# Linear attention and a maxout layer on one core: batch 0 reordered, w2 @ w_out by one Strassen level, copies and relus moved to ScalarE

## The chip, the cores and the metric

The kernel runs on one core of one Trainium2 chip. The metric is the device time in microseconds (us) of one execution, the median of several. The core has five engines with queues of their own, each working through its instructions in order: TensorE (PE: matmuls, and loads of their weights, PEld), VectorE (DVE), ScalarE (ACT), GpSimd (POOL, here issuing loads) and SyncE (SP, issuing stores and transposing transfers). They wait for each other through semaphores.

## The reference

```python
# q, k, v: (8, 8, 1024, 64) f32;  E, F: (64, 1024);  w1, w2: (512, 1024);  w_out: (1024, 512)
k_proj = einsum('ks,bhsd->bhkd', E, k)
v_proj = einsum('ks,bhsd->bhkd', F, v)
scores = q @ k_proj^T / 8
attn   = softmax(scores)                       # over 64 projected keys
x      = (attn @ v_proj) -> (8192, 512)        # heads side by side
g      = maximum(x @ w1, x @ w2)               # (8192, 1024)
out    = g @ w_out                             # (8192, 512)
```

## The kernel before

The maxout is rewritten. With wd = w1 - w2 it is max(x @ w1, x @ w2) = relu(x @ wd) + x @ w2, and so

    out = relu(x @ wd) @ w_out + x @ (w2 @ w_out)

The product m = w2 @ w_out (512 x 512) is formed once. Each batch is two units of 512 tokens. For a unit there is an "up" product x @ wd, then a relu, and a "down" product [g, x] @ [w_out; m]. All down products, and the up products from unit 2 on, are computed by one level of Strassen's method (the Winograd form): a 2 x 2 block product with 7 block products in place of 8, and sums of blocks before and after, made by DVE. Batch 0's up products are plain matmuls. Everything runs in f16 with f32 accumulation in PSUM.

The instructions are recorded in an order that the kernel fixes itself. Batch 0, as it stands at the head:

```python
    step_dn(t, 0, 1)              # sums of exp(scores), then Ln on ACT
    step_inv(t, 0, 0)             # Exp(-ln): the reciprocal
    step_inv(t, 0, 1)
    warm(4)                       # 4 matmuls of 512 columns that keep the PE clock up
    step_qt(t, 4, 4, 0, NI // 2)  # transposes of q on PE, copy on DVE
    step_qt(t, 4, 4, NI // 2, NI)
    warm(2)
    step_sc(t, 1, 0)              # scores on PE, Exp on ACT
    step_sc(t, 1, 1)
    step_kv(t, 0, 4, "v")         # projection of the first half of v
    step_dn(t, 1, 0)
    step_at(t, 0, 0)              # values on PE, times the reciprocal on DVE: x
    step_dn(t, 1, 1)
    step_at(t, 0, 1)
    step_inv(t, 1, 0)
    step_kv(t, 4, 8, "v", True)
    step_inv(t, 1, 1)
    step_wd(0, 0, 2)              # wd = w1 - w2, a first piece, on DVE
    step_at(t, 1, 0, True)
    u0, u1 = [*up_slots(t, 0)], [*up_slots(t, 1)]
    step_wd(0, 2, 4)
    step_at(t, 1, 1, True)
    for u in u0, u1:
        for x in u[0:2]:
            x(r1=2)               # first half of the contraction of four up products
```

Then come the up products of batch 0, the transposes of w2 and the product m:

```python
    # in up(): 4 matmuls of 512 columns into one PSUM bank, then the relu into SBUF
                if fb < 3 or j and fb > 3:
                    nc.scalar.activation(out=gt[:, fb, :], in_=h_ps, func=ACTF.Relu)
                else:
                    nc.vector.tensor_scalar_max(gt[:, fb, :], h_ps, 0.0)

    def step_w2t(f0):             # 8 transposes into one bank, one copy on ACT
        ps_t = mm_bank(FP16)
        ...
    def step_m(r):                # one of four row blocks of m
        m_ps = mm_bank(n=(1, 2, 0, 3)[r])
        for fb in range(NFB):     # NFB = 8
            nc.tensor.matmul(
                out=m_ps, lhsT=w2t_sb[:, fb, r * 128 : (r + 1) * 128], rhs=wo_sb[:, fb, :],
                start=(fb == 0), stop=(fb == NFB - 1),
            )
        nc.scalar.copy(out=m_sb[:, r, :], in_=m_ps)

    slots = [
        (0, lambda: u0[0](r0=2)), (1, lambda: u0[1](r0=2)), (None, lambda: loads(1, "v", "q", "k")),
        (2, lambda: u1[0](r0=2)), (3, lambda: u1[1](r0=2)),
        (None, wd[1]), (4, u0[2]), (None, wt[0]), (5, u0[3]),
        (None, wd[2]), (None, wt[1]), (6, u1[2]), (7, u1[3]), (None, wt[2]), (None, wt[3]), (8, u0[4]), (9, u0[5]), (None, wd[3]),
        (10, u1[4]), (11, u1[5]), (12, u0[6]), (13, u0[7]),
        (14, u1[6]), (15, u1[7]),
        *((16 + n, lambda n=n: step_m(n)) for n in range(NDC)),     # NDC = 4
    ]
```

Steps of DVE are hung on these slots: sums of blocks of x (`sums_x`) and of g (`sums_g`), differences of blocks of w_out and m (`step_t` into `T_sb`) and of wd (`step_tw`):

```python
    for key, s_, *a in (
        (10, open_box, 1), (11, sums_x, U[0, 0], (2,)), (12, sums_x, U[0, 0], (0,)),
        (13, sums_x, U[0, 0], (1,)), (14, sums_x, U[0, 0], (3,)), (15, open_box, 0, 2),
        (15, sums_g, U[0, 0], (0, 1)), (16, step_t, 0), (16, sums_g, U[0, 0], (2, 3)),
        *((17 + i // 3, step_tw, i) for i in range(4)), (19, open_box, 3),
    ):
        at_slot((0, key), s_, *a)
```

A unit's down product comes in seven parts p1 to p7 of 12 matmuls of 256 columns, in unit 0 cut into two pieces each. Banks X, Y and Z hold the partial results. Some are copied to SBUF (`keep`), some are read from PSUM by an addition on DVE whose result is stored:

```python
        def keep_d(bank):         # unit 0: on VectorE; other units: on ScalarE
            return keep("pd", bank, *([nc.vector.tensor_copy] if u["n"] == 0 else []))
        def p1(): st["s1"] = keep_d(whole(1, "X", xbank))
        def p2(): add(0, 0, whole(2, "Y", ybank), st["s1"])
        def p6(): st["u1"] = keep_d(whole(6, "X", None))       # goes on in bank X
        def p5(): st["s5"] = keep_d(whole(5, "Z", ybank))      # takes Y's bank: needs p2's addition done
        ...
```

Batch 1's attention (projection of k and v, transposes, scores, sums, values) is hung on the pieces of unit 0, that of later batches on those of later units. From batch 2 on, q is transposed by transfers that SyncE issues. The loads of the batch after next are held back by a one-element copy on GpSimd (`step_gate`) that waits for such a transfer.

Of the kernel before, what the change touches and what calls it, by code (L numbers as in the profile page):

```python
# [16 lines left out]
def kernel(  # L17
# [12 lines left out]
    nc = tc.nc  # L30
# [146 lines left out]
        t["qt"] = qtp.tile([128, H, HALF], FP16, tag="qt", name="qt_sb")  # L177


    def step_kv(t, h0=0, h1=H, which="kv", att=False, dma=False):  # L180
        kv_ps = att_banks()[:, 0, :] if att else mm_bank()
        n = (h1 - h0) * D
        both = which == "v"
        for c in range(NC):
            for w in which:
                i = "kv".index(w)
                for r in range(2) if both else (i,):
                    nc.tensor.matmul(  # L188
                        out=kv_ps[r * KP : (r + 1) * KP, 0:n],
                        lhsT=eft[:, i, c, :],  # L190
                        rhs=t[w][:, h0:h1, c, :],
                        start=(c == 0), stop=(c == NC - 1),
                    )
        fl = lambda ap: ap[:, h0:h1].rearrange("p h z d -> p (h z d)")
        zd = lambda ap: ap.rearrange("p (h d z) -> p h z d", d=D // 2, z=2)
        if "k" in which:
            eng = nc.vector.tensor_copy if which == "k" else nc.scalar.copy
            kp = t["kp"][:, h0:h1]
            eng(out=kp[:, :, 0, :], in_=kv_ps[0:KP, 0:n].rearrange("p (h d) -> p h d", d=D))
        if both:  # L200
            eng = nc.scalar.copy if att else nc.vector.tensor_copy
            eng(out=t["vp"][:, h0:h1], in_=zd(kv_ps[:, 0:n]))
        elif "v" in which:
            def finish_v():
                nc.vector.tensor_copy(out=t["vp"][KP:128, h0:h1], in_=zd(kv_ps[KP:128, 0:n]))
                if dma:
                    nc.vector.tensor_copy(out=kp[:, :, 1, :], in_=kp[:, :, 0, :])
                    step_kpt_dma(t)
                nc.vector.tensor_copy(out=fl(t["vp"][0:KP]), in_=fl(t["vp"][KP:128]))

            if att:
                return finish_v
            finish_v()
# [110 lines left out]
        ld = t["ld", g, j]  # L324
        nc.scalar.activation(out=ld, in_=ld, func=ACTF.Exp, scale=-1.0)

    def step_at(t, g, j, att=False):
        if "xt" not in t:
            new_xt(t)
        ld = t.pop(("ld", g, j))  # L330
        if att:
            both = att_banks()
            at_ps = [both[:, o, :] for o in range(2)]
        else:
            at_ps = [mm_bank() for _ in range(2)]
        values_into(t, g, j, at_ps)
        for o in range(2):
            nc.vector.tensor_tensor(
                out=x_out(t, g, j)[:, :, o, :],
                in0=at_ps[o].rearrange("q (z n) -> q z n", z=2),  # L340
                in1=ld[:, o, None, :].broadcast_to([128, 2, W]),
                op=ALU.mult,
            )
# [63 lines left out]
    def up_slots(t, j):  # L407
        t["gt", j] = gt = gpool.tile([128, NFB, HALF], FP16, tag="gt", name="gt_sb")
        for fb in range(NFB):
            def up(fb=fb, r0=0, r1=NDC):  # L410
                if r0 == 0:
                    t["up", j, fb] = mm_bank()
                h_ps = t["up", j, fb]
                for r in range(r0, r1):
                    nc.tensor.matmul(  # L415
                        out=h_ps,
                        lhsT=wd_sb[:, r, fb * 128 : (fb + 1) * 128],
                        rhs=t["xt"][:, r, :, j * W : (j + 1) * W],
                        start=(r == 0), stop=(r == NDC - 1),
                    )  # L420
                if r1 < NDC:
                    return
                if fb < 3 or j and fb > 3:
                    nc.scalar.activation(out=gt[:, fb, :], in_=h_ps, func=ACTF.Relu)
                else:
                    nc.vector.tensor_scalar_max(gt[:, fb, :], h_ps, 0.0)
            yield up
# [5 lines left out]
            in1=w2_sb[:, r0:r1, f0 : f0 + 256], op=ALU.subtract,  # L433
        )

    def step_w2t(f0):
        ps_t = mm_bank(FP16)
        for f in range(2):
            for r in range(NDC):
                nc.tensor.transpose(  # L440
# [5 lines left out]
        nc.scalar.copy(  # L446
            out=w2t_sb[:, fb : fb + 2, :].rearrange("q f m -> q (f m)"), in_=ps_t
        )

    def step_m(r):  # L450
        m_ps = mm_bank(n=(1, 2, 0, 3)[r])
        for fb in range(NFB):
            nc.tensor.matmul(  # L453
                out=m_ps, lhsT=w2t_sb[:, fb, r * 128 : (r + 1) * 128], rhs=wo_sb[:, fb, :],
                start=(fb == 0), stop=(fb == NFB - 1),
            )
        nc.scalar.copy(out=m_sb[:, r, :], in_=m_ps)

# [29 lines left out]
    def step_t(part, which=range(4)):  # L490
# [4 lines left out]
            lambda h, c: src[:, h * hs : (h + 1) * hs, c * CH : (c + 1) * CH], which,  # L495
        )

    def s_g(i):
        return box[2].rearrange("q (s n m) -> q s n m", s=4, n=NG)[:, i]

# [20 lines left out]
        return u["gt"][:, h * NG : (h + 1) * NG, j * W : (j + 1) * W]  # L521


    def step_s(u, blk, S, which):
        for i in which:
            x, y, op = (
                (blk(u, 1, 0), blk(u, 1, 1), ALU.add),
                (S(0), blk(u, 0, 0), ALU.subtract),
                (blk(u, 0, 0), blk(u, 1, 0), ALU.subtract),
                (blk(u, 0, 1), S(1), ALU.subtract),  # L530
            )[i]
            nc.vector.tensor_tensor(out=S(i), in0=x, in1=y, op=op)  # L532

    def sums_x(u, which):
        step_s(u, x_blk, lambda i: s_x(i, u), which)
# [87 lines left out]
    def down_steps(u, alone):  # L623
# [49 lines left out]
            nc.vector.tensor_tensor(out=o_sb, in0=two(x), in1=two(y), op=ALU.add)  # L673
            store(j, c, o_sb)

        def keep_d(bank):
            return keep("pd", bank, *([nc.vector.tensor_copy] if u["n"] == 0 else []))

        size = 2 * (NG + NX) // (1 if alone else 2 if u["n"] == 0 else 3)

        def piece(k, name, n, m):
# [3 lines left out]
            return product(k, name, n, 2 * (NG + NX) - size)  # L685

        def p1():
            st["s1"] = keep_d(whole(1, "X", xbank))

        def p2():  # L690
            add(0, 0, whole(2, "Y", ybank), st["s1"])

        def p6():
            st["u1"] = keep_d(whole(6, "X", None))

        def p5():
            st["s5"] = keep_d(whole(5, "Z", ybank))

        def p7():
            st["u2"] = keep_d(whole(7, "X", None))  # L700
            if alone:
                add(1, 1, st["u2"], st["s5"])

# [46 lines left out]
    step_dn(t, 0, 1)  # L750
    step_inv(t, 0, 0)
    step_inv(t, 0, 1)
    warm(4)
    step_qt(t, 4, 4, 0, NI // 2)
    step_qt(t, 4, 4, NI // 2, NI)
    warm(2)
    step_sc(t, 1, 0)
    step_sc(t, 1, 1)
    step_kv(t, 0, 4, "v")
    step_dn(t, 1, 0)  # L760
    step_at(t, 0, 0)
    step_dn(t, 1, 1)
    step_at(t, 0, 1)
    step_inv(t, 1, 0)
    step_kv(t, 4, 8, "v", True)
    step_inv(t, 1, 1)
    step_wd(0, 0, 2)
    step_at(t, 1, 0, True)
    u0, u1 = [*up_slots(t, 0)], [*up_slots(t, 1)]
    step_wd(0, 2, 4)  # L770
    step_at(t, 1, 1, True)
    for u in u0, u1:
        for x in u[0:2]:
            x(r1=2)


    load_all(tiles[1], 1, "k", k)
# [4 lines left out]
    def loads(b, *names):  # L782
# [15 lines left out]

    slots = [
        (0, lambda: u0[0](r0=2)), (1, lambda: u0[1](r0=2)), (None, lambda: loads(1, "v", "q", "k")),  # L800
        (2, lambda: u1[0](r0=2)), (3, lambda: u1[1](r0=2)),
        (None, wd[1]), (4, u0[2]), (None, wt[0]), (5, u0[3]),
        (None, wd[2]), (None, wt[1]), (6, u1[2]), (7, u1[3]), (None, wt[2]), (None, wt[3]), (8, u0[4]), (9, u0[5]), (None, wd[3]),
        (10, u1[4]), (11, u1[5]), (12, u0[6]), (13, u0[7]),
        (14, u1[6]), (15, u1[7]),
        *((16 + n, lambda n=n: step_m(n)) for n in range(NDC)),
    ]
    slots = [((0, n), x) for n, x in slots]

# [3 lines left out]
    for n, key in enumerate(units):  # L813
# [4 lines left out]
            continue  # L818
        pieces = [(("P", n, p, i), x) for p, x in enumerate(downs) for i, x in enumerate(x)]
        ups = [*up_steps(U[units[n + 1]])]  # L820
        for h, (x, y) in enumerate(((5, 1), (1, 2)) if n == 1 else ((2, 2), (2, 3))):
            slots += pieces[:x]
            slots.append((("G", n, h), lambda: None))
            slots += pieces[x : x + y]
# [11 lines left out]


    for key, s_, *a in (
        (10, open_box, 1), (11, sums_x, U[0, 0], (2,)), (12, sums_x, U[0, 0], (0,)),
        (13, sums_x, U[0, 0], (1,)), (14, sums_x, U[0, 0], (3,)), (15, open_box, 0, 2),  # L840
        (15, sums_g, U[0, 0], (0, 1)), (16, step_t, 0), (16, sums_g, U[0, 0], (2, 3)),
        *((17 + i // 3, step_tw, i) for i in range(4)), (19, open_box, 3),
    ):
        at_slot((0, key), s_, *a)


    t = tiles[1]
    at_slot((0, 19), new_attn, t)
    at_slot((0, 19), lambda: turn.__setitem__(slice(None), [2, 3]))
    for n, x in enumerate((  # L850
        "", "", "kv", "", "kpt", "qt00 qt10", "", "sc00 sc10", "qt01", "qt11", "",
        "dn00 in00 dn10 in10", "", "", "at00 AT10 sc01",
    )):
        key = ("P", 0, (n - 1) // 2, (n - 1) % 2) if n else (0, 19)
        for name in x.split():
            if name[0] == "k":
                if name == "kpt":
# [9 lines left out]
                at_slot(key, s_, t, *args, *([True] if name[:2] == "AT" else []))  # L867
        if n in (1, 5):
            at_slot(key, step_t, 1, (0, 1) if n == 1 else (2, 3))
        if 6 <= n < 10:  # L870
            at_slot(key, sums_x, U[0, 1], ((2, 0, 1, 3)[n - 6],))


    t = tiles[2]
    at_slot(("P", 0, 1, 0), new_attn, t)
    at_slot(("P", 0, 1, 0), step_qt_dma, t, 0, H // 2)
    at_slot(("U", 1, 0, 1), step_kv, t, 0, H, "kv", True)
    at_slot(("U", 1, 0, 4), step_kpt, t, 0, H, True)
    at_slot(("G", 1, 0), step_qt_dma, t, H // 2, H)
    at_slot(("U", 1, 0, 6), step_gate, t, "qt", H // 2 - 1)  # L880
    at_slot(("U", 1, 0, 6), loads, 3, "k", "v", "q")

    for b in range(3, B):
# [20 lines left out]
    for n, (b, o) in enumerate(units):  # L904
# [2 lines left out]
        if b == 0:  # L907
            where = ()
        elif n == 2:
            where = (("P", 1, 0, 2), 0), (("P", 1, 1, 0), 1), (("P", 1, 1, 1), 2), (("U", 1, 0, 1), 3)  # L910
        else:
            where = tuple((("U", n - 2, 1, k), i) for k, i in ((6, 2), (3, 0), (4, 1), (5, 3)))
        for key, i in where:
# [48 lines left out]
```

The softmax here doesn't subtract the row's maximum and nothing guards it: scores larger than these inputs give would overflow.

## Time and profile before

| | |
|---|---|
| time, median of 3 runs | 325.81 us (325.14 to 325.97) |
| span of the profiled run | 323.2 us |
| granted TensorE clock | 1.00 |
| matmul of 512 columns in a row of such, start to start (6.91 us / 32) | 0.216 us |
| matmul of 256 columns, four in 0.44 us | 0.109 us |
| ACT copy or relu, 128x512 f32 from PSUM | 0.59 to 0.60 us |
| DVE relu, 128x512 f32 from PSUM | 0.69 us |
| DVE sum or difference, 128x1024 f16 | 0.69 us |
| product m on PE | 40.01 to 46.91 us |

How to read it: the page gives each engine's busy time in the span. Matmuls overlap in a pipeline, so one matmul's own duration (0.273 us for 256 columns) is longer than the distance between two. The chain that ended last is followed back from the last instruction, at each step to what released it; the waits say which engine stood idle until another's instruction or a transfer ended. "issue" is time for which the profile shows no cause.

### The profile page before, as it was taken

The page shows a single profiled execution, that of the slowest core. Times are in us where ns is not written, and L with a number is a line of the kernel's source. Part 1 is how long each engine was busy: PE and PEld are TensorE (multiplying, and loading weights), DVE is VectorE, ACT ScalarE, POOL GpSimd, SP SyncE. Part 2 cuts the span into 40 slices and gives each one's busy share as a digit, 9 for nine tenths or more (in the row PEclk, how much of TensorE's full clock was granted, in tenths as well). Part 3 has the DMA queues.
Part 4 walks back from the last instruction along what each step waited for, and adds up shares of the span by engine and source line. Part 5 has one row for each costly group of instructions (what it writes and reads, how often), then busy time and mean ns, then how long its engine had stood idle before and what let it go on. Part 6 is the DMA issues. An engine that isn't in the chain of part 4 may idle for free.

```text
span 323.2 us, 9033 instructions
## 1 busy us (share of the span) xinstructions
PE 316.0 (98%) x3852; PEld 248.4 (77%) x3852; DVE 236.8 (73%) x420; ACT 203.1 (63%) x364; POOL 41.6 (13%) x65
## 2 busy tenths in 40 slices
PE   8989999999999999999999999999999999999995
PEld 3554457878887888878887888878887888888884
DVE  1365798896867797877967796977967796969572
ACT  1466532667676777667776777657776777764541
POOL 8649002001200300030000300030000000000000
PEclk9999999999999999999999999999999999999999
DMA  8999999999999799699979999689969130312133
GB/s 160 207 196 185 204 204 204 207 203 179 256 216 213 135 203 244 143 177 144 234 147 201 154 211 231 115 180 183 232 130 213 38 100 32 99 34 98 34 121 108
DMA packets 76280, 53.14 MB, mean 164 GB/s; under 512 B 29520, under 2 KB 76112, under 8 KB 76240
## 3 DMA queue, kind: packets, MB, share of 16 engines
q0 software_dynamic: 30976, 28.31, 56.0%
q1 hardware_dynamic: 45264, 24.25, 31.2%
q8 instruction: 30, 0.49, 0.6%
q14 instruction: 10, 0.08, 0.1%
HBM read 57.15 MB, written 16.78 MB: 229 GB/s over the span
## 4 chain that ended last, share of the span: by engine, by line
PE 84%; DMA 9%; DVE 2%; POOL 2%; issue 1%; SPq 1%; ACT 0%; DVEq 0%; POOLq 0%
PE mm_ps L649 43%; PE mm_ps L571 24%; PE att_ps L188 4%; DMA v_sb<-in_v_dram 4%; DMA qt_sb<-q_sb 3%; PE mm_ps L415 3%; PE att_ps L287 3%; PE mm_ps L275 3%; PE mm_ps L453 2%; DMA big<-in_moe_w_dram 2%; POOL q_sb L102 1%; POOL k_sb L102 1%; DVE gt_sb L586 1%; PE mm_ps L246 1%; PE mm_ps L440 1%
## 5 line engine op out<-in xcount | busy, mean ns | idle before, releaser
L542 ACT COPY p_sb<-mm_ps 128x512 f32<-128x512 f32 x172 | 97.2, 594 | 42.0 <-PE mm_ps L571 30.0
L649 PEld LDWEIGHTS <-big 128*128 128x128 f16 x768 | 73.5, 98 | 12.0 <-issue 3.5
L649 PE MATMUL mm_ps<-T_sb,big 128*128 128x256 f16 x576 | 77.9, 273 | 0.0
L586 DVE TENSOR_TENSOR gt_sb<-mm_ps,p_sb 128x512 f16<-128x512 f32 x56 | 38.6, 688 | 45.5 <-PE mm_ps L571 42.7
L571 PE MATMUL mm_ps<-big,big 128*128 128x256 f16 x336 | 50.4, 273 | 0.0
L571 PEld LDWEIGHTS <-big 128*128 128x128 f16 x448 | 43.8, 98 | 5.2
L649 PEld LDWEIGHTS <-gt_sb 128*128 128x128 f16 x384 | 35.8, 98 | 9.9 <-issue 5.4
L649 PE MATMUL mm_ps<-wo_sb,gt_sb 128*128 128x256 f16 x256 | 43.0, 273 | 0.1
L571 PEld LDWEIGHTS <-wd_sb 128*128 128x128 f16 x336 | 32.9, 98 | 3.8
L571 PE MATMUL mm_ps<-xt_sb,wd_sb 128*128 128x256 f16 x224 | 33.6, 273 | 0.0
L364 ACT ACTIVATE ex_sb<-mm_ps 128x512 f16<-128x512 f32 x50 | 27.2, 597 | 10.2 <-PE att_ps L287 8.1
L390 DVE TENSOR_TENSOR xt_sb<-att_ps,ld_sb 128x1024 f16<-128x1024 f32 x26 | 31.7, 1219 | 0.1
L673 DVE TENSOR_TENSOR o_sb<-mm_ps,p_sb 128x512 f32<-128x512 f32 x32 | 21.9, 685 | 7.7 <-PE mm_ps L649 7.7
L649 PE MATMUL mm_ps<-m_sb,xt_sb 128*128 128x256 f16 x128 | 24.4, 273 | 0.0
L238 POOL COPY junk<-qt_sb 1x1 f16<-1x1 f16 x6 | 1.7, 284 | 169.6 <-DMA qt_sb<-q_sb 169.6
L621 ACT ACTIVATE gt_sb<-mm_ps 128x512 f16<-128x512 f32 x28 | 16.8, 600 | 8.7 <-PE mm_ps L571 8.7
L532 DVE TENSOR_TENSOR big<-gt_sb 128x1024 f16<-128x1024 f16 x32 | 21.9, 685 | 0.3
L589 DVE TENSOR_SCALAR gt_sb<-gt_sb 128x512 f16<-128x512 f16 (+1 forms) x56 | 20.4, 365 | 1.9
L649 PE MATMUL mm_ps<-wo_sb,big 128*128 128x256 f16 x128 | 21.5, 273 | 0.0
L649 PE MATMUL mm_ps<-T_sb,gt_sb 128*128 128x256 f16 x128 | 21.5, 273 | 0.0
L649 PEld LDWEIGHTS <-xt_sb 128*128 128x128 f16 x192 | 18.8, 98 | 2.2
L586 DVE TENSOR_TENSOR gt_sb<-p_sb 128x512 f16<-128x512 f32 x28 | 19.1, 682 | 0.0
(88 smaller groups left out, 429.5 us busy)
## 6 DMA issues: line engine op xcount, KB each, us to landing
out_dram<-o_sb SPq DMA_DIRECT2D x63, 256.0 KB, 2.7
k_sb<-in_k_dram POOLq DMA_DIRECT2D x7, 1024.0 KB, 11.3
v_sb<-in_v_dram POOLq DMA_DIRECT2D x7, 1024.0 KB, 16.7
q_sb<-in_q_dram POOLq DMA_DIRECT2D x5, 1024.0 KB, 22.8
q_sb<-in_q_dram POOLq DMA_DIRECT2D x4, 512.0 KB, 19.4
big<-in_moe_w_dram POOLq DMA_DIRECT2D x12, 128.0 KB, 8.6
k_sb<-in_k_dram POOLq DMA_DIRECT2D x4, 256.0 KB, 6.1
q_sb<-in_q_dram POOLq DMA_DIRECT2D x4, 256.0 KB, 7.2
```

Source lines behind the costliest of these rows:

```text
L188: nc.tensor.matmul(out=kv_ps[r * KP : (r + 1) * KP, 0:n], lhsT=eft[:, i, c, :], rhs=t[w][:, h0:h1, c, :], start=(c == 0), stop=(c == NC - 1),)
L275: nc.tensor.matmul(out=banks[e][pos : pos + Z, h * W : (h + 1) * W], lhsT=t["kpt"][o * D : (o + 1) * D, head, s * Z : (s + 1) * Z], rhs=t[ ...
L364: nc.scalar.activation(out=t["ex", g, j][:, e, :], in_=banks[e], func=ACTF.Exp, scale=scale)
L390: nc.vector.tensor_tensor(out=x_out(t, g, j).rearrange("q z o n -> q o z n"), in0=at_ps.rearrange("q o (z n) -> q o z n", z=2), in1=ld[:, ...
L532: nc.vector.tensor_tensor(out=S(i), in0=x, in1=y, op=op)
L542: copy(out=x, in_=bank)
L571: nc.tensor.matmul(out=bank[:, m * W : (m + 1) * W], lhsT=w_[:, n_, (2 * d + m) * 128 : (2 * d + m + 1) * 128], rhs=a[:, n_, :], start=(n ...
L586: nc.vector.tensor_tensor(out=c_blk(j, c), in0=two(x), in1=two(y), op=ALU.add)
L589: nc.vector.tensor_scalar_max(ap, ap, 0.0)
L621: nc.scalar.activation(out=out, in_=in_, func=ACTF.Relu)
L649: nc.tensor.matmul(out=bank[:, i * CH : (i + 1) * CH], lhsT=a(c)[:, i * 128 : (i + 1) * 128], rhs=w_(c), start=(n is not None and m == (lo ...
L673: nc.vector.tensor_tensor(out=o_sb, in0=two(x), in1=two(y), op=ALU.add)
```

## The change

It has these parts:

- **m by Strassen.** m = w2 @ w_out is computed as seven block products of 8 matmuls of 256 columns (56 in all) in place of 32 matmuls of 512 columns. It needs four sums of blocks of w2 transposed and three additions at the end, on DVE; four partial results are copied to SBUF by ScalarE, and a fifth goes straight to m. It uses the differences of w_out's blocks that the down products use anyway, so these are formed earlier.
- **Head of batch 0.** Four warm-up matmuls fall away. The projection of v's first half comes ahead of the last scores, values ahead of sums, and a first piece of wd is formed between two multiplications. Two of the four groups of w2's transposes move ahead, into the banks of the attention.
- **Relus and copies.** In batch 0 all relus but the two of block 3 run on ScalarE; unit 0's partial results are copied by ScalarE instead of VectorE.
- **Batch 1 two pieces later**, counted in pieces of unit 0; in unit 1 the first block of attention comes one piece later.
- **Batch 2.** The first transposing transfer of q is issued after the first store's place, and the loads of batch 3 are gated on the second of these transfers instead of the first.

It is meant to shorten PE's stream and to keep the engines around it from holding it up.

```diff
-                if fb < 3 or j and fb > 3:
+                if fb != 3:
                     nc.scalar.activation(out=gt[:, fb, :], in_=h_ps, func=ACTF.Relu)
...
-    def step_m(r):
-        (8 matmuls of 512 columns, one copy)
+    def sums_m(i):
+        m_sums[i] = ppool.tile([128, NG, CH], FP16, tag="pd", bufs=4, name="p_sb")
+        sum_s(lambda j, h: m_blk(j, h), lambda n: m_sums[n], i)
+    def m_steps():
+        def product(k, name, n):          # 8 matmuls of 256 columns
+            ...
+        def p1(): st["s1"] = keep("pu", product(1, "X", 3))
+        def p2(): add(0, 0, product(2, "Y", 1), st["s1"])
+        def p6(): st["u1"] = keep("pu", product(6, "X", None))
+        def p5(): st["s5"] = keep("pu", product(5, "Z", 1))
+        def p7(): st["u2"] = keep("pu", product(7, "X", None))
+        def p3():
+            add(0, 1, product(3, "Z", None), st["u1"])
+            add(1, 1, st["u2"], st["s5"])
+        def p4(): nc.scalar.copy(out=block(1, 0), in_=two(product(4, "X", None)))
+        return [p1, p2, p6, p5, p7, p3, p4]
...
-        def keep_d(bank):
-            return keep("pd", bank, *([nc.vector.tensor_copy] if u["n"] == 0 else []))
-            st["s1"] = keep_d(whole(1, "X", xbank))
+            st["s1"] = keep("pd", whole(1, "X", xbank))
...
-    warm(4)
     step_qt(t, 4, 4, 0, NI // 2)
     step_qt(t, 4, 4, NI // 2, NI)
     warm(2)
     step_sc(t, 1, 0)
+    step_kv(t, 0, 4, "v")
     step_sc(t, 1, 1)
-    step_kv(t, 0, 4, "v")
+    step_at(t, 0, 0)
     step_dn(t, 1, 0)
-    step_at(t, 0, 0)
+    step_at(t, 0, 1, between=lambda: step_wd(0, 0, 2))
     step_dn(t, 1, 1)
-    step_at(t, 0, 1)
+    step_kv(t, 4, 8, "v", copy=nc.scalar.copy)
     step_inv(t, 1, 0)
-    step_kv(t, 4, 8, "v", True)
+    step_at(t, 1, 0, True)
     step_inv(t, 1, 1)
-    step_wd(0, 0, 2)
-    step_at(t, 1, 0, True)
...
+    step_w2t(0, True)                      # after the first halves of the up products
...
+        (None, lambda: step_w2t(256, True)),
         (2, lambda: u1[0](r0=2)), (3, lambda: u1[1](r0=2)),
-        (None, wd[1]), (4, u0[2]), (None, wt[0]), (5, u0[3]),
-        (None, wd[2]), (None, wt[1]), (6, u1[2]), ...
+        (None, wd[1]), (4, u0[2]), (5, u0[3]),
+        (None, wd[2]), (6, u1[2]), ...
-        *((16 + n, lambda n=n: step_m(n)) for n in range(NDC)),
+        *((16 + n, x) for n, x in enumerate(m_steps())),
...
-        for h, (x, y) in enumerate(((5, 1), (1, 2)) if n == 1 else ((2, 2), (2, 3))):
+        for h, (x, y) in enumerate(((6, 1), (1, 1)) if n == 1 else ((2, 2), (2, 3))):
...
-        (10, open_box, 1), (11, sums_x, U[0, 0], (2,)), (12, sums_x, U[0, 0], (0,)),
-        (13, sums_x, U[0, 0], (1,)), (14, sums_x, U[0, 0], (3,)), (15, open_box, 0, 2),
-        (15, sums_g, U[0, 0], (0, 1)), (16, step_t, 0), (16, sums_g, U[0, 0], (2, 3)),
-        *((17 + i // 3, step_tw, i) for i in range(4)), (19, open_box, 3),
+        *((10 + i // 2, sums_m, i) for i in range(4)), *((12 + i, step_t, 0, (i,)) for i in range(4)),
+        (15, open_box, 0, 1, 2), (16, sums_x, U[0, 0], range(4)),
+        (18, sums_g, U[0, 0], (0, 1)), (19, sums_g, U[0, 0], (2, 3)), (22, open_box, 3),
...
-        "", "", "kv", "", "kpt", "qt00 qt10", ...
+        "", "", "", "", "kv", "", "kpt", "qt00 qt10", ...
...
-    at_slot(("P", 0, 1, 0), step_qt_dma, t, 0, H // 2)
+    at_slot(("P", 0, 2, 0), step_qt_dma, t, 0, H // 2)
-    at_slot(("U", 1, 0, 6), step_gate, t, "qt", H // 2 - 1)
+    at_slot(("U", 1, 0, 6), step_gate, t, "qt", H - 1)
```

## The prediction

> **What bounds the kernel now.** I read the page's busy shares first, then a table by stage, then the waits of TensorE (PE), and last the chain of work in time. The busy shares and the granted clock:
>
> ```profile
> PE 316.0 (98%) x3852; PEld 248.4 (77%) x3852; DVE 236.8 (73%) x420; ACT 203.1 (63%) x364; POOL 41.6 (13%) x65
> ...
> PEclk9999999999999999999999999999999999999999
> ```
>
> TensorE is busy in 98% of the span at full clock. So TensorE's instruction stream sets the time, and a change pays only if it shortens that stream or closes one of its few gaps. The table by stage shows where gaps are; its columns are the stretch, its length, and busy us (instructions) of PE, weight loads (PEld), DVE, ACT and POOL:
>
> ```profile
> 18.00:24.00 6.00, 4.55 (x145) 2.77 (x130) 3.88 (x8) 4.44 (x7) 3.25 (x5) 1.00 1.37 194
> 24.00:40.00 16.00, 15.86 (x97) 7.95 (x96) 10.16 (x19) 8.80 (x13) 7.77 (x10) 1.00 1.28 194
> 40.00:47.00 7.00, 7.00 (x36) 3.27 (x34) 6.90 (x12) 2.41 (x5) 0.00 (x0) 1.00 1.26 206
> 47.00:62.00 15.00, 15.00 (x244) 11.56 (x241) 11.80 (x24) 5.68 (x9) 2.37 (x3) 1.00 1.31 205
> ```
>
> Only 18 to 24 us has real holes (1.45 us). From 40 to 47 us, the product w2 @ w_out, PE has none, and DVE (6.90 of 7.00) is as full as PE. The waits of PE up to 110 us, in total us, times, longest:
>
> ```profile
> PE att_ps L287 <- ACT vp_sb L202: 0.5, 1, 0.5
> PE mm_ps L415 <- DVE wd_sb L431: 0.4, 1, 0.4
> ...
> PE mm_ps L275 <- DMA qt_sb<-q_sb: 0.3, 1, 0.3
> ```
>
> These are all small. The chain in time (start, length, what) says what lies beneath them:
>
> ```profile
> 8.35 12.82 DMA v_sb<-in_v_dram
> ...
> 26.94 0.70 DVE wd_sb L431
> ...
> 33.10 6.91 PE mm_ps L415 x32
> 40.01 6.91 PE mm_ps L453 x32
> 46.91 1.09 PE mm_ps L649 x10
> ```
>
> The head hangs on the second half of v, which lands at 8.35 + 12.82 = 21.17 us, and then on a weight piece (DVE forms w1 - w2 from it at 26.94). From 27.7 us on PE is the chain.
>
> **What the Trainium skill says.** "TensorE: Matmul & The Clock Gate", section Back-to-back issue gap, gives 262 cycles for 256 columns and 518 for 512 at 2.4 GHz: 109 and 216 ns. This trace agrees: 6.91 us / 32 = 216 ns for L453, and a 4-matmul group of 256 columns takes 0.44 us. Part 1 of the same page says that the clock falls after some 3.4 us without work; the granted clock here is 1.00 in every stage though PE sat idle in pieces, so dropping warm-up matmuls should not cost clock. "ScalarE: Activation LUTs", Rules for kernel authors, wants relu on VectorE. For these f32 PSUM sources the trace says otherwise: 600 ns on ScalarE, 690 ns on VectorE. "VectorE: DVE Perf Modes", the perf-mode tier table, puts two-tensor operations at double rate from 16-bit SBUF and single from PSUM; the trace agrees (1024 f16 elements 0.69 us, 512 f32 from PSUM 0.69 us).
>
> **The change part by part.**
>
> *The product m = w2 @ w_out.* Before: 4 groups of 8 matmuls of 512 columns, 32 x 216 ns = 6.91 us. After: 7 products of 8 matmuls of 256 columns, 56 x 109 ns = 6.11 us. Gain 0.80 us of PE time, all on the path. The rest of the instruction counts confirms it: PE loses 32 matmuls and 4 warm-ups and gains 56, and nothing else.
>
> *What Strassen adds elsewhere.* DVE gets 4 sums of w2 blocks (4 x 0.69 = 2.7 us) and 3 additions (3 x 0.69 = 2.1); it loses 4 relus and unit 0's 4 copies (8 x 0.69 = 5.5). ACT gets 4 copies for m (4 x 0.59), 4 relus (4 x 0.60) and unit 0's 4 copies (4 x 0.59), and loses the 4 copies of m (4 x 0.59) but keeps one for the last block: about +7.7 - 2.4 = +5.3 us between 25 and 62 us, where it has been busy about 8.8 of 16, 2.4 of 7 and 5.7 of 15. Both engines stay under PE's length, so the totals fit; the order is what can hurt.
>
> *The head, 15 to 40 us.* Dropping 4 warm-ups (0.86 us) brings the transposes of q forward, but the first half of v lands at 18.7 (issued at 7.59, 11.1 to landing) and the second at 21.17 as before, and the new order puts the projection of v in front of the second score. So PE waits for v instead. I walked the chain on with the timeline's durations (exp 1.02 us on ACT, logarithm 0.60, copy of v 0.37, values 0.6 on PE): values at 20.4, exp of the late score 20.1 to 21.1, two logarithms to 22.25, the copy of v to 22.85, values to 23.5, up-projection at about 23.6 (before: 23.80). DVE now forms the first w1 - w2 ahead of the last multiplication, so it is ready by 23.2. After that two groups of 8 transposes (0.45 us each) are pulled ahead of the wait for the weight piece and fill the 0.42 us wait on wd_sb. The PE work up to m is equal, 64 x 216 ns + 32 transposes x 56 ns = 15.6 us, so m starts at about 39.4 instead of 40.0. Gain 0.6 us.
>
> *The wait I expect in its place.* The weights w_out are issued at 26.72 and take 11.3 us:
>
> ```profile
> L138 POOL DMA_DIRECT2D wo_sb<-in_moe_w_out_dram x1: 907/907/907, 26.7 to 26.7; - x1
> ...
> DMA to landing us min/median/max: 11.3/11.3/11.3
> ```
>
> That is 38.0 us. In the new DVE order the four differences of w_out's blocks (T) come right after the sums of w2, which are ready by about 36.6 (the last transposes end at 32.2, two copies on ACT of 1.01 us each make 34.2, four sums 0.60 apart follow), so DVE waits for 38.0. Then four T take, start to start,
>
> ```profile
> 41.12 0.69 DVE L488 TENSOR_TENSOR T_sb<-wo_sb 128x1024 f16<-128x1024 f16 x1
> ...
> 43.65 0.69 DVE L532 TENSOR_TENSOR big<-gt_sb 128x1024 f16<-128x1024 f16 x1
> ```
>
> 43.65 - 41.12 = 2.53 us, to 40.6. Four sums of x (0.42 each, about 1.65 in all) follow to 42.25, and only then the first addition of m, 0.69 us, to 42.95. This addition frees the PSUM bank into which the fourth product (p5) starts. PE would like to start p5 at 39.4 + 24 x 0.109 = 42.0. So p5 starts at about 43.0, a wait of 1.0 us. The four last products take 4 x 0.87 = 3.5 us: m ends at 46.5 instead of 46.91. Of the 1.4 us won by then 0.4 is left. The end of m is tied to the landing of w_out and DVE's queue, not to the head.
>
> *Unit 0 and batch 1.* Same PE work and as many switches between kinds. In the old order the k/v projection of batch 1 ran at 48.15, just when v had landed (28.64 + 19.5 = 48.1); two pieces later, from 46.5, it runs at 49.1 and waits for nothing. DVE still has a queue (m's last additions, T, four differences of wd) when the scores need the copies of q: I allow 0.2 us of new wait.
>
> *Batch 2.* The third load of k is gated on both transposing transfers of q instead of the first. The second then no longer shares the DMA engines with that load (it took 10.66 us from 72.17), so the 0.3 us wait at 82.9 goes. The first took 66.67 to 71.82, 5.2 us; at that length the second ends near 78, and k, v and q of batch 3 go out then (before: k at 73.0, v at 83.4). Gain 0.3 us.
>
> Sum: -0.6 - 0.8 + 1.0 + 0.2 - 0.3 = -0.5 us if the wait for w_out is as I work it out; -1.5 us without it. I hold the wait for somewhat more likely than not and put the middle at -0.8: 325.81 - 0.8 = 325.0.
>
> **The rivals.**
> 1. *No wait in m: the full 1.4 us is kept, about 324.3.* For it: PE waits for DVE nowhere in this region before, and the sums of x may run quicker. Against it: DVE is 99% full here before and its work now has to be done before, not after, the products.
> 2. *ScalarE becomes the bound in the up-projection.* It takes 14 relus x 0.60 + 4 copies x 1.01 = 12.4 us between 25 and 40, against 16 groups x 0.86 us of PE; by my walk a bank comes free near 29.7 just when PE wants it. For it: ACT's queue is in order and starts late, at 26. Against it: VectorE keeps the two relus where the copies crowd, and ACT gains 0.26 us per group. If wrong, up to 1 us in the head, which m's wait would partly hide: 325 to 326.
> 3. *The later order collides in unit 1*, where DVE is busy 17.36 of 21 us: the additions of unit 1 now fall beside the copies for batch 2. For it: little slack. Against it: PE waited for no engine there before. Cost up to 1 us: 326.
> 4. *A transfer turns late*: batch 3's k goes out 5 us later. It is needed at 102.7; loads of k took 9.3 to 14.8 us to land there, and 78 + 15 = 93, so no.
>
> **Range and chances.** The measured runs before spread from 325.14 to 325.97, which already adds 0.4 each way. Rival 1 with the noise gives 323.9; rivals 2 or 3 give 326.1. A gain over 2% (6.5 us) would need more PE time than the change touches; a loss over 2% would need a long new stall in a kernel in which every moved transfer has slack.
>
> **What would show it.** Right: 56 matmuls of m in place of 32, PE's waits listing a wait of some 1 us of an m product on the addition into m_sb, m starting near 39.4 and unit 0 near 46.5, no wait on qt_sb near 83, clock 1.00. Wrong: unit 0 starting at 45.5 (no wait), or at 47 or later (the DVE chain longer, or ACT late with its relus); new waits of PE between 50 and 80 us; a time outside the range would most likely come from there.

## The result and the profile after

The changed kernel takes 330.27 us in the median of six runs (329.23 to 337.4), the kernel before 325.81 us (325.12 to 327.21). The ratio is 1.0139, with a 95% interval of 1.0102 to 1.0176. It is slower by 4.5 us, where 0.8 us less had been predicted. The run that was profiled is the longest of the six, and a second transfer came late in it; what is read from it below is held against the traces of the experiments.

The page of the changed kernel: busy shares, granted clock, and one line of its table of DMA queues (packets, MB, share of 16 engines) that is needed at the end:

```profile
PE 318.6 (95%) x3872; PEld 252.5 (75%) x3872; DVE 236.6 (70%) x419; ACT 208.5 (62%) x373; POOL 41.1 (12%) x65
...
PEclk9999999999999799997899999999999999999999
...
q8 instruction: 30, 0.49, 0.6%
```

PE's busy share falls from 98% to 95%, and the clock has two dips where it had none: one in the 14th slice (109 to 117 us; a slice is 8.4 us), one in the 19th and 20th. PE's waits, the one that is new and the one that was predicted (total us, times, longest):

```profile
PE mm_ps L274 <- DMA kpt_sb<-kp_sb: 8.4, 3, 4.3
...
PE mm_ps L517 <- DVE m_sb L530: 0.2, 1, 0.2
```

The scores (L274) wait in three places for kpt, the transposed projection of k. The first is in batch 3, and the chain of work there (start, length, what) has the transfer just ahead of the score:

```profile
109.39 1.21 DVE gt_sb L647 x2
...
110.99 2.84 DMA kpt_sb<-kp_sb
...
113.87 0.63 PE mm_ps L274 x9
```

The chain puts an addition on DVE (gt_sb) and a store ahead of the transfer; what had held SyncE until then is seen below. PE's score starts at 113.87 us, when the transfer has landed. Before, it started at 110.21 us,

```profile
110.21 0.62 PE L275 MATMUL mm_ps<-qt_sb,kpt_sb 64*32 64x256 f16 x16
```

and the transfer had landed at 109.7 us. The transfer is no slower (2.8 us to landing, before 2.7); it is issued later. SyncE's timeline before (start, length of the issue, line, operation):

```profile
100.17 5.70 SPq L258 DMA_TRANSPOSE qt_sb<-q_sb  x2
105.96 0.53 SPq L664 DMA_DIRECT2D out_dram<-o_sb  x1
106.97 1.20 SPq L232 DMA_TRANSPOSE kpt_sb<-kp_sb  x1
```

and after:

```profile
105.45 4.39 SPq L257 DMA_TRANSPOSE qt_sb<-q_sb  x2
109.94 0.94 SPq L725 DMA_DIRECT2D out_dram<-o_sb  x1
110.99 1.23 SPq L231 DMA_TRANSPOSE kpt_sb<-kp_sb  x1
```

The order is the same: two transposing transfers of batch 3's q, a store, then k's. The three start 4.0 to 5.3 us later. SyncE's own waits from 96 to 112 us, before

```profile
SPq L258 <- DMA q_sb<-in_q_dram: 0.6, 1, 0.6
...
SPq L232 <- DVE kp_sb L207: 0.4, 1, 0.4
```

and after, say what held the first:

```profile
SPq L257 <- DMA q_sb<-in_q_dram: 6.3, 1, 6.3
```

SyncE waits 6.3 us for the load of batch 3's q (before, 0.6 us). Before, it had then stood 0.4 us for the copy of k (kp_sb) that k's transfer reads; afterwards nothing of that slack is left. So the next question is when q's load went out. GpSimd's timeline before:

```profile
73.04 0.90 POOL L102 DMA_DIRECT2D k_sb<-in_k_dram  x1 [0.62 <-PE mm_ps L571]
83.40 0.87 POOL L102 DMA_DIRECT2D v_sb<-in_v_dram  x1 [9.46 <-DMA qt_sb<-q_sb]
84.27 0.88 POOL L102 DMA_DIRECT2D q_sb<-in_q_dram  x1
```

and after:

```profile
79.95 0.90 POOL L102 DMA_DIRECT2D k_sb<-in_k_dram  x1 [1.05 <-PE mm_ps L632]
80.84 0.88 POOL L102 DMA_DIRECT2D v_sb<-in_v_dram  x1
81.70 0.90 POOL L102 DMA_DIRECT2D q_sb<-in_q_dram  x1
```

The load of q is issued 2.6 us earlier than before and still lands 5 us later. Before, k had gone out at 73.04 us, and q landed 15.8 us after its own issue. Now k, v and q go out one behind the other, and q lands 23.7 us after its issue, at 105.4 us. In the kernel before, too, where the three loads go out together (batches 4 to 7), q's takes 22.3 to 23.1 us; its line there (KB, median us to landing, with batch 3's 15.8 us among the five):

```profile
q_sb<-in_q_dram POOLq DMA_DIRECT2D x5, 1024.0 KB, 22.8
```

Until the loads went out in the changed kernel, the DMA engines had stood nearly idle: their busy share from 78 to 80 us is 0.04, before 0.86. In the table by stage (the last columns are the clock, the DMA share and GB/s) the kernel before has

```profile
78.00:84.00 6.00, 5.69 (x87) 4.71 (x86) 5.90 (x12) 3.57 (x8) 0.60 (x1) 1.00 1.09 181
```

and the changed one

```profile
78.00:84.00 6.00, 6.00 (x90) 5.05 (x89) 5.90 (x12) 3.95 (x9) 2.83 (x4) 1.00 0.35 64
108.00:114.00 6.00, 2.15 (x47) 1.53 (x52) 3.02 (x5) 1.24 (x3) 1.31 (x4) 0.99 0.96 193
114.00:120.00 6.00, 6.00 (x55) 4.51 (x45) 1.28 (x3) 3.74 (x7) 1.67 (x2) 0.73 0.98 136
```

The gate's price is in the first row: 64 GB/s in place of 181, since the loads start only at 79.95 us. The second row is PE's wait. The third shows its sequel: PE is busy for 6.00 us of 6.00, but at a clock of 0.73. The clock is at half speed from 113.8 to 117.2 us. The distance from batch 3's first score to its next one shows what that costs: 9.88 us here, 8.51 us before, so 1.4 us.

**The sum in batch 3.** PE reached the k/v projection of batch 3 at 102.30 us (before 102.67), so in this trace 0.37 us had been gained. Then come a wait of 3.85 us and 1.4 us of half clock: 3.85 + 1.4 - 0.37 = 4.9 us, for 4.5 us measured. Experiment e7 below runs the same instructions up to there, without the second late transfer: projection at 102.67 us, a wait of 3.2 us, 9.77 us between the scores, so 3.2 + 1.3 = 4.5 us, for 4.2 us measured.

**The second place**, batch 4, is peculiar to the profiled run. Here the transfer is not issued late but lands late, 7.7 us after its issue:

```profile
L231 SPq DMA_TRANSPOSE kpt_sb<-kp_sb x1: 1597/1597/1597, 147.8 to 147.8; - x1
...
  PE mm_ps L274: 4.3, 1
...
DMA to landing us min/median/max: 7.7/7.7/7.7
```

PE waits 4.3 us for it, and the clock is at half speed for another 6.8 us.

### The profile page after: what moved, and what is told of

It reads as the page before. It is cut to its first block, busy times and chain, and to the rows that moved or that the text cites. A ratio compares the mean times of both kernels' runs of the same rounds, so it can differ in the third digit from the quotient of the medians.

```text
span 335.6 us, 9084 instructions
## 1 busy us (share of the span) xinstructions
PE 318.6 (95%) x3872; PEld 252.5 (75%) x3872; DVE 236.6 (70%) x419; ACT 208.5 (62%) x373; POOL 41.1 (12%) x65
## 4 chain that ended last, share of the span: by engine, by line
PE 79%; DMA 11%; DVE 4%; POOL 4%; issue 1%; ACT 0%; SPq 0%; DVEq 0%; POOLq 0%
PE mm_ps L710 43%; PE mm_ps L632 25%; DMA kpt_sb<-kp_sb 4%; DMA v_sb<-in_v_dram 4%; PE att_ps L188 4%; DMA wo_sb<-in_moe_w_out_dram 3%; PE mm_ps L274 3%; PE att_ps L286 3%; POOL big L134 1%; PE mm_ps L517 1%; DVE gt_sb L647 1%; POOL q_sb L102 1%; POOL k_sb L102 1%; DVE T_sb L480 1%; DVE big L589 1%
## 5 line engine op out<-in xcount | busy, mean ns | idle before, releaser
L603 ACT COPY p_sb<-mm_ps 128x512 f32<-128x512 f32 x180 | 102.1, 592 | 50.3 <-PE mm_ps L632 31.4
L710 PEld LDWEIGHTS <-big 128*128 128x128 f16 x768 | 74.9, 100 | 14.2 <-issue 4.3
L710 PE MATMUL mm_ps<-T_sb,big 128*128 128x256 f16 x576 | 80.5, 279 | 0.0
L632 PEld LDWEIGHTS <-big 128*128 128x128 f16 x448 | 43.8, 98 | 5.3 <-issue 0.2
L632 PE MATMUL mm_ps<-xt_sb,wd_sb 128*128 128x256 f16 x224 | 34.7, 279 | 0.2 <-ACT ex_sb L365 0.2
L274 PE MATMUL mm_ps<-qt_sb,kpt_sb 64*32 64x256 f16 x400 | 11.1, 284 | 8.4 <-DMA kpt_sb<-kp_sb 8.4
```

The source lines that it names most:

```text
L274: nc.tensor.matmul(out=banks[e][pos : pos + Z, h * W : (h + 1) * W], lhsT=t["kpt"][o * D : (o + 1) * D, head, s * Z : (s + 1) * Z], rhs=t[ ...
L603: copy(out=x, in_=bank)
L632: nc.tensor.matmul(out=bank[:, m * W : (m + 1) * W], lhsT=w_[:, n_, (2 * d + m) * 128 : (2 * d + m + 1) * 128], rhs=a[:, n_, :], start=(n ...
L710: nc.tensor.matmul(out=bank[:, i * CH : (i + 1) * CH], lhsT=a(c)[:, i * 128 : (i + 1) * 128], rhs=w_(c), start=(n is not None and m == (lo ...
```

## The experiments

The theory, called A in the expectations, is that the loss comes from the gate alone: it delays batch 3's loads, q comes last of them, and k's transfer stands behind q's in SyncE's order. The rival, B, puts the loss into the rest of the change. The labels e1 to e11 are the ones that the expectations use. "Before" in each line below is the kernel before, timed beside the experiment.

**Gate put back, all else as changed (e1).**

```diff
-    at_slot(("U", 1, 0, 6), step_gate, t, "qt", H - 1)
+    at_slot(("U", 1, 0, 6), step_gate, t, "qt", H // 2 - 1)
```

> The changed kernel with one line undone: the loads of batch 3 are gated on the first transposing transfer of q again, not on the second. Theory A (the gate holds the load of k back, the DMA engines stand idle near 78 to 84 us, so q of batch 3 lands some 5 us late, its transposing transfers and, behind them in SyncE's queue, that of k are late): the wait of PE on kpt_sb near 110 us is gone, clock 1.000, time 324.9 to 325.5. Theory B (the two pieces by which batch 1 and the loads of batch 2 come later are enough to lose the race): a wait on kpt_sb of 1 us or more stays, time 326.5 or more.

325.30 us against 325.39 us, ratio 0.9997 (0.9979 to 1.0015): the loss is gone, the clock is 1.00. What is left of PE's waits in the part that the prediction worked out:

```profile
PE mm_ps L517 <- DVE m_sb L530: 0.8, 1, 0.8
```

B falls. The rest of the change is worth nothing that can be measured in this form. In this trace the transfer of batch 3's k lands at 110.15 us and the score starts at 110.26 us; the one of batch 6 takes 3.6 us.

**The gate alone, in the kernel before (e2).**

```diff
-    at_slot(("U", 1, 0, 6), step_gate, t, "qt", H // 2 - 1)
+    at_slot(("U", 1, 0, 6), step_gate, t, "qt", H - 1)
```

> The kernel before with only the gate's line changed: the loads of batch 3 wait for the second transposing transfer. Theory A: 329.5 to 331, a wait of PE on kpt_sb of 3.5 to 4.5 us near 110 us, mean clock 0.995, a DMA hole near 78 to 84 us. Theory B: within 0.5 us of before, no such wait.

330.39 us against 325.39 us, ratio 1.0144 (1.0104 to 1.0184): one argument of one line makes the whole loss. PE's wait in this kernel:

```profile
PE mm_ps L275 <- DMA kpt_sb<-kp_sb: 3.6, 1, 3.6
```

The DMA share from 78 to 84 us is 0.33, and the distance between batch 3's first two scores is 9.97 us. Batch 4's transfer lands in 2.7 us here. So the loss needs neither Strassen's m nor the second late transfer of the changed kernel's profile. One of the six runs, at clock 1.00, took 327.26 us; the other five had a mean clock of 0.990 to 0.995.

**Half of q's transfer behind k's, in batch 3 (e5).** If the order of SyncE's queue passes the delay on, k's transfer ahead of q's second half must shorten the wait.

```diff
         at_slot(key, step_qt_dma, t, 0, H // 2)
-        at_slot(key, step_qt_dma, t, H // 2, H)
+        if b > 3:
+            at_slot(key, step_qt_dma, t, H // 2, H)
         at_slot(("U", n, 0, 1), step_kv, t, 0, H, "kv", True, True)
+        if b == 3:
+            at_slot(("U", n, 0, 4), step_qt_dma, t, H // 2, H)
```

> The changed kernel with the second half of batch 3's transposing transfer of q put behind that of k in SyncE's queue; the gate stays on the second transfer. If k's transfer is late because it stands behind q's in the queue (part of theory A): it goes out some 2 to 3 us earlier, PE waits on kpt_sb for about 1 us, the clock stays 1.000, time 325.5 to 327. If k itself is late: the wait stays near 3.9 us and the time near 329.8.

SyncE's timeline:

```profile
105.75 1.93 SPq L257 DMA_TRANSPOSE qt_sb<-q_sb  x1
...
108.83 1.23 SPq L231 DMA_TRANSPOSE kpt_sb<-kp_sb  x1
```

k's transfer goes out 2.2 us earlier, PE's wait in batch 3 falls from 3.85 to 1.29 us, and the clock does not drop there. This part came as expected. The time did not: 330.47 us, ratio 1.0148 (1.012 to 1.0176). In batch 4 PE waited 2.77 us, and the clock fell there instead. Two things came together. The transfer took 4.3 us in place of 2.7. And it was issued 1.9 us after its copy of k was ready (144.05 us, issue at 145.97): the loads of batch 4 are gated on q's second half of batch 3, which now came later, so they went out at 115.29 us (changed kernel 113.05), and SyncE again stood waiting for q's load, for 4.2 us. So the experiment shows the queue's part in the wait, and that the delay went on to the next batch by the same path; the total time alone tells nothing for or against A.

**PE kept busy through the wait (e3).** Sixteen matmuls of 512 columns, whose result nobody reads, ahead of the score that waits. This separates the wait from what the clock adds to it.

```diff
+        if (n, h) == (3, 1):
+            at_slot(("G", n, h), fill, 16)
         at_slot(("G", n, h), step_group, *new, *old)
```

> The changed kernel with 16 matmuls of 512 columns (3.5 us) put on PE just ahead of the place where it waits for kpt_sb, so that PE works through most of the wait; nothing else changes, the 16 results are not used. If the idle stretch also costs clock (the mean granted clock is 0.995 after it, 0.5% of 328 us = 1.6 us): clock 1.000 and 1.3 to 2 us less than the changed kernel, about 328.2. If the lower clock is only a mark of the wait: the same 329.8, or more.

The stage again:

```profile
108.00:114.00 6.00, 6.00 (x43) 3.92 (x40) 4.32 (x7) 2.28 (x5) 0.39 (x3) 1.00 1.11 225
114.00:120.00 6.00, 6.00 (x88) 4.82 (x87) 2.00 (x3) 4.01 (x8) 2.59 (x3) 1.00 0.71 106
```

The clock stays at 1.00, and the distance between the scores is 8.31 us in place of 9.88. So the drop follows from the idle time, and without it the 1.4 us between these scores are not lost. The time, 331.67 us, ratio 1.0182 (1.0137 to 1.0227), missed again: in the profiled run (333.84 us) batch 4's transfer took 6.3 us, PE waited 2.9 us, and the clock fell there. But the three runs of the six in which the clock stayed at 1.00 took 329.35 to 330.62 us, about as much as the changed kernel's runs. What the drop costs the whole kernel is therefore not shown; the 1.4 us are read from the distance of two scores.

**Later loads behind k's transfer (e7).** Is that other late landing caused by the loads of the next batch, which go out 0.58 us behind the transfer in batch 4?

```diff
-        at_slot(("U", n, 0, 6), step_gate, t, "kp", H - 1, 1)
+        at_slot(("U", n, 0, 6), step_gate, t, "kpt", H - 1)
```

> The changed kernel with its gate on q's second transfer kept, and from batch 3 on the next loads gated on the landed transfer of k (kpt_sb) instead of on the copy that it reads, so that no load starts while k is transposed. If the long landing in batch 4 (7.7 us in the changed kernel's profile) needs the loads beside the instruction fetch: k's transfer of batch 4 lands in 2.7 to 4.4 us whatever the fetches do; the wait of batch 3 (3.9 us) stays; time 329 to 331, no run above 333. If the fetch alone makes it: 6 us and more again where a 16 KB fetch begins within 2.2 us.

Batch 4's transfer lands in 2.7 us. The wait in batch 3 stays (3.2 us, clock 0.995), and the time is 330.02 us, ratio 1.0142 (1.0116 to 1.0168). So the second late transfer is not what makes the median slow: this kernel hasn't got it, and loses as much. Whether the loads had made it late stays open: in the kernel before they went out 0.6 us behind the same transfer, and it landed in 2.8 us.

**The gate alone, with 20 more small matmuls at the start (e9).** Do more PE instructions alone move the late landings?

```diff
     warm(8)
+    (20 matmuls of 64 columns into a bank of their own)
```

> The kernel of e2 (before, with the gate's line alone) with 20 more matmuls of 64 columns in the first warm-up, where PE waits for loads: as many more matmuls as the changed kernel has. In the traces so far k's transfer took 3.6 to 7.7 us instead of 2.7 in exactly the six cases (of 28) where an instruction fetch of 16 KB began within 2.2 us of its issue; the fetches move with PE's instruction count. If that is the cause of the changed kernel's second wait: here k's transfer of batch 4 or 6 takes 3.6 us or more, a second wait of PE on kpt_sb appears in batch 4 in some runs, and the time lies above e2's 330.4, at 331 to 335. If not: as e2, 330.4.

329.45 us, ratio 1.0137 (1.011 to 1.0164). Batch 6's transfer took 4.0 us, as expected, and PE waited 0.6 us for it. But the whole stream is late from the start. The first projection of k, before

```profile
8.21 1.06 PE L188 MATMUL mm_ps<-k_sb,eft 128*64 128x256 f16 x8
```

and here:

```profile
10.34 1.92 PE L193 MATMUL mm_ps<-k_sb,eft 128*64 128x256 f16 x8
```

It starts 2.1 us later, and unit 0 starts 3.5 us later (50.27 us, before 46.75). The added matmuls account for 1.2 us of that. The rest comes of slower matmuls: the projection takes nearly twice as long, and so do the others up to 14.2 us (two warm-up matmuls 1.03 us, before 0.61), although the clock column shows 1.00. Batch 3's wait vanished behind that. The expected time was missed, and the loss here is another one: a late start, not the gate.

**Plain m, gate put back (e4).** The 32 matmuls of 512 columns return, and the sums of w2's blocks fall away; the slots behind m are renumbered to match.

```diff
-        *((16 + n, x) for n, x in enumerate(m_steps())),
+        *((16 + n, lambda n=n: step_m(n)) for n in range(NDC)),
...
-        *((10 + i // 2, sums_m, i) for i in range(4)), *((12 + i, step_t, 0, (i,)) for i in range(4)),
+        *((12 + i, step_t, 0, (i,)) for i in range(4)),
```

> The changed kernel with the gate back (as in e1) and m computed as before: 32 matmuls of 512 columns, no sums of w2's blocks. By the prediction's arithmetic Strassen saves 0.80 us of PE and, through the wait on the addition (0.8 us in e1's trace, 0.2 in the changed kernel's), gives back 0.2 to 0.8: m takes 6.9 us on PE and unit 0 starts 0 to 0.6 us later than in e1; time 325.3 to 325.9. If the part is worth more than its wait costs: at least 0.6 us slower than e1.

m takes 6.91 us, and unit 0 starts at 46.42 us, with Strassen's m (gate put back) at 46.53 us. So Strassen's 0.8 us do not reach unit 0: the wait in m takes them. The time is 326.69 us against 325.77 us, ratio 1.0026 (1.0008 to 1.0044), over the expected 325.9, with a wait of 1.3 us on q's transfer in batch 2.

**Sums of x behind m's first addition, gate put back (e6).** This takes away what makes PE wait in m.

```diff
-        (15, open_box, 0, 1, 2), (16, sums_x, U[0, 0], range(4)),
+        (15, open_box, 0, 1, 2), (17, sums_x, U[0, 0], range(4)),
```

> The kernel of e1 with DVE's four sums of x put behind the first addition of m instead of ahead of it. If the wait in m is, as predicted, PE waiting for DVE's queue (w_out landing, four T, four sums of x, then the addition): PE's wait on m_sb is gone, unit 0 starts some 0.2 to 0.8 us earlier after m's start, time 324.6 to 325.1. If the bank is late for another reason: the wait stays at 0.8 us.

m takes 6.26 us with no wait inside, and unit 0 starts at 45.70 us, 0.8 us earlier. The time is 326.01 us, ratio 1.0027 (1.0002 to 1.0051): no gain, and the expected time was missed. In this trace PE comes to batch 2 before q has been transposed:

```profile
PE mm_ps L274 <- DMA qt_sb<-q_sb: 1.0, 1, 1.0
```

The next kernel, the same up to there, reached batch 2 at 81.98 us without such a wait, so it does not come in every run.

**Three attempts at a better order (e8, e10, e11).** The first puts half of q's transfer behind k's in every batch from 3 on, on top of the kernel just shown:

```diff
-        at_slot(key, step_qt_dma, t, H // 2, H)
         at_slot(("U", n, 0, 1), step_kv, t, 0, H, "kv", True, True)
+        at_slot(("U", n, 0, 4), step_qt_dma, t, H // 2, H)
```

> The kernel of e6 and, for every batch from 3 on, the second half of the transposing transfer of q behind that of k in SyncE's queue, so that the next batch's loads (gated on that second half) start after k's transfer has landed. If k's transfer is late where loads or instruction fetches run beside it: it lands in 2.7 to 2.8 us in every batch, at most 3.6 where an instruction fetch of 16 KB falls on it; no wait of PE on kpt_sb; time 324.3 to 325.0. Against: the second half of q comes some 3 us later and may be waited for.

327.54 us, ratio 1.0052 (1.0029 to 1.0074). 324.3 to 325.0 had been expected. In the profiled run PE reaches batch 3 at 101.78 us, 0.9 us earlier than before, and waits 1.3 us for late landings of k in batches 4 and 6 (4.4 and 3.7 us), though no load goes out near them. That run took 325.48 us; what the others, 2 us longer in the median, lost is in no trace. The second adds the changed kernel's gate again, and issues batch 3's loads as k, half of q, v, half of q:

```diff
+        load_all(tiles[3], 3, "k", k)
...
+        load(tiles[3], "q", q, 3, 0, H // 2)
+        load(tiles[3], "v", v, 3, 0, H)
+        load(tiles[3], "q", q, 3, H // 2, H)
```

> The candidate of e8 with the gate of the changed kernel on q's second transfer for batch 3, and batch 3's loads in the order k, first half of q, v, second half of q, so that what is needed first lands first. If the order in which the loads land is what the gate broke: no wait of PE on qt_sb in batch 2 and none above 0.3 us on kpt_sb in batch 3, though the DMA hole at 78 to 84 us is there again; time 324.5 to 326.5. If the hole itself is the loss: a wait of 2 us or more on kpt_sb or on v stays.

326.71 us, ratio 1.0037 (1.0021 to 1.0053), just above the expected 326.5. With the gate in place and q's first half ahead of v, batch 3's wait for k is 0.5 us in place of 3.85, and the wait on q in batch 2 is gone: the gate is dear through the order in which the loads behind it land. (Half of q stands behind k here as well; that alone had left 1.3 us.) Another wait for k in batch 6 (1.4 us) and 1.5 us for v in the head remain. The third is the second with the plain m, and q's transfer split in batch 3 alone:

> As e10, but with m in 32 matmuls as before (and only batch 3's second half of q behind k's transfer), so that PE's instruction count and with it the place of the instruction fetches is near that of the kernel before. Expected: no fetch within 2.2 us of a transfer of k, all of them 2.7 to 2.8 us, no wait on qt_sb or kpt_sb above 0.3 us; time 324.6 to 325.5, that is 0.3 to 0.8 us less than before. If the order of loads doesn't help: 326 or more.

327.56 us, ratio 1.0082 (1.0049 to 1.0115). The profiled run, at 329.75 us one of the longer ones, has 3.2 us of waits for k and a clock drop. This expectation was missed. No version beat the kernel before.

## Why the prediction was wrong, step by step

- **m's length.** 56 x 109 = 6.11 us was predicted. Where nothing waits inside, m takes 6.26 us. Right.
- **The head.** m was to start at 39.4 us. It starts at 39.44 us with the gate put back, and at 39.72 us in the changed kernel's trace, where v's first half, which landed at 19.1 us and not at 18.7, kept PE waiting 1.9 us. Right, within 0.3 us, and in part by luck: the sum as written, 23.6 + 15.6 us, gives 39.2 and not 39.4, and the up-projection started at 24.1 us in that trace.
- **The wait in m.** 1.0 us was predicted; 0.8 us with the gate put back, 0.2 us in the changed kernel, where m began later. Unit 0 was to start at 46.5 us, tied to w_out's landing. It starts at 46.53 and at 46.22 us, each time 8.24 us after DVE's first difference of w_out (38.29 and 37.98 us). Right, and rival 1 falls.
- **Rival 2** (ScalarE in the up-projection) and **rival 3** (a collision in unit 1): no such wait is among the long ones; every trace of the new order has one of 0.2 us in unit 1, on ScalarE (ex_sb), which the kernel before has not. But of the 0.53 us gained at unit 0 and the 0.3 us of batch 2 only 0.37 us were left at batch 3's projection: 0.46 us lost on the way, where 0.2 us was allowed. And in four other traces whose instructions up to there are the same, or differ in the gate alone, nothing was left (102.64, 102.67, 102.73 and 103.63 us, before 102.67). Where the rest went is not shown.
- **Batch 2.** The wait on q's transfer at 82.9 us is gone, as predicted. The step that failed is the other half of this term, that k, v and q go out then at no cost, and with it **rival 4**, which took the danger up and dismissed it. It asked when batch 3's k is needed, took a landing of k by 93 us, and compared it with 102.7 us. That holds: k landed at 93.5 us. But the last of the three to land is the third, q, and it came 5.3 us later than before (100.1 and 105.4 us). Its next user is SyncE, which had already waited 0.6 us for it before the change. Behind q's transposing transfers in SyncE's in-order queue stands k's, with 0.4 us to spare, and behind that PE, with 0.5 us. With k going out at 78 us, q's load follows at about 80; with some 22.8 us, as in batches 4 to 7 of the trace before, it lands near 102.6 us (an estimate), over 2 us later than before. All these numbers were in the trace of the kernel before. The claim that "every moved transfer has slack" was made without looking up the last user of each.
- **Clock 1.00.** Right for the warm-ups, wrong once PE stood still for 3.85 us. "TensorE: Matmul & The Clock Gate", Part 1, gives a free-running window of 3413 ns, with half clock after an idle one. The traces agree on the window: within each, all changes of the clock lie whole multiples of 3.41 us apart. On the condition they differ. Counted in these windows, the seven drops behind waits each came after a window in which PE had stood idle for 2.0 to 3.4 us (2.0 in the gate alone, 2.1 in the last experiment), while windows with up to 1.6 us idle brought none, the wait of 1.9 us in the head among them, since it falls across two. So a wait's length alone does not decide. Only two drops near 8 us, at the start of e5 and e6, came with less than 0.5 us idle ahead of them; they stay unexplained.

So the gain up to unit 0 was worked out nearly right, 0.4 us of it or nothing was left at batch 3, and a term put at -0.3 us cost 5.3 us (3.85 of waiting, 1.4 of half clock). The loss stayed within 2%, but the text gave a late transfer no weight.

## What to carry to other kernels

When a load is gated or delayed, follow each load behind the same gate, the last one above all, to its user, and from there down the in-order queue of whatever engine issues the next transfer, to the compute engine; then hold the delay against the margins on that path. A transfer that lands 0.5 us before it is used is all but a bound, although PE's waits don't list it. And an idle TensorE can cost more than its idle time: 3.85 us of waiting cost 1.4 us of half clock on top, read between two scores.

## What was not expected of the hardware

The transposing transfer of k takes 2.6 to 3.1 us to land, but in 14 of 65 cases 3.2 to 7.7 us. In the packets of the traces nearly all the slow ones share one thing. The page's "q8 instruction" row lists 30 packets of 16 KB, taken here for the fetches of PE's instructions; such a packet takes 0.9 to 2.0 us. Of the transfers that were slow, all but one (3.8 us) had such a fetch starting within 2.2 us after their issue, and none of the others had. In the kernel before and in the one with the gate alone no transfer had one, and all landed in 2.7 to 2.8 us. The limit of 2.2 us is drawn from these cases: fetches 2.26 to 2.37 us after the issue went with 2.7 to 2.8 us. The loads of the next batch do not decide it: where they went out 0.6 us behind a slow transfer, it took anything from 3.6 to 7.7 us, and with no load near, 3.2 to 4.4 us. "Runtime: NRT & Kernel Launch", section Instruction fetch mechanics, tells of blocks of 16 KiB on a DMA queue of the engine's own, at a cost that is mostly hidden. The blocks and the queue are seen here; whether the cost is hidden from a transfer that such a fetch meets is what these traces put in doubt. Where the fetches fall moves with the number of PE instructions: the changed kernel has 20 more matmuls, each with a weight load, and the fetch at 219.2 us before is at 215.7 us with the gate put back. This is a coincidence in time over thirteen traces, not a test: no kernel held the fetches in place and moved the transfer alone, so the cause stays likely and not shown.
